# A fifth unit of the sequence transform as seven block products in six of its eight passes, with one gate/up unit more made late, and two GpSimd steps instead of four for one pair's sums

## The chip, the cores and the metric

The kernel runs on one core of a Trainium2 chip. The metric is the device time of one execution in microseconds (us), measured on the chip from outside the program. One more execution is taken by the hardware profiler; all rows of the profile and the trace quoted below come from it. Engines: PE (TensorE matmul) and PEld (its weight loads), DVE (VectorE), ACT (ScalarE), POOL (GpSimd), SP (SyncE, which here issues all the DMAs).

## The reference

A Fourier mixing layer and a GeGLU feed-forward layer, each behind a layer norm and with a residual, for one sequence of S = 2048 rows of width D = 448; the hidden width of the second layer is 1792.

```python
a = jnp.einsum("bsd,ed->bse", x, dft_hid_re)
b = jnp.einsum("bsd,ed->bse", x, dft_hid_im)
y = jnp.einsum("ts,bse->bte", dft_seq_re, a) - jnp.einsum("ts,bse->bte", dft_seq_im, b)
...
x = A_x
h = x + _A_ref(_layernorm(x, axis=-1), ...)
g = jnp.einsum("bsd,df->bsf", x, w_gate)
u = jnp.einsum("bsd,df->bsf", x, w_up)
h2 = h + einsum(gelu(g) * u, w_down)      # g and u of layernorm(h)
```

## The kernel before

All products are made in fp16 with both factors split into a high part and a low remainder (`hi_part` on ACT, `lo_part` on DVE), and three of the four products of the parts are summed: each product of the reference is three matmuls. The schedule is written out by hand or by a planner in the kernel's own code; no compiler moves an instruction.

**The Fourier stage** takes the first half. A hidden transform F(i) turns one tile of 128 rows of x (normed, split, transposed: `x_stats`, `x_rstd_steps`, `x_lo`, `x_turn`) into the tile's features: 22 matmuls of 448 columns at line 456, into two banks of a ring of PSUM (tag `"B"`, so that F(3) takes the banks that F(0) had). `feature_high` (ACT) and `feature_low` (DVE) then read the banks and write the operand tile `b0`, `b1`, ...

The sequence transform follows in 8 passes p of 8 units u. A unit U(p, u) multiplies one 512 KB block of the sequence matrix, `wr`, with the operand tiles of the pair 2u, 2u+1 and adds to the pass's four banks `acc` (line 573). A **plain** unit is 24 matmuls of 448 columns, with `ws` = high and low of all four blocks of `wr` (`seq_high`, `seq_low`, 128x1024 each). A unit of `S_UNITS` = (4, 5, 6, 7) is made from **seven block products**: 42 matmuls of 224 columns. It needs three sums of blocks (`seq_sums`, lines 517 to 521, into `wsum`), high and low of only three blocks of `wr` (`seq_parts`: 128x256 and 128x512), and high and low of the four sums (`seq_high_s`, `seq_low_s`, 128x1024, into `wss`). On the side of the features such a pair goes through a ring tile `b32` in fp32, three sums (`feature_sums`, lines 493 to 497), and high and low of seven blocks (`sums_high`, `sums_low`, 128x1568).

The stage also does other work beside the matmuls: the residual, norm and transposes of a finished pass (`seq_out`, `ffn_...`), and 12 of the 14 units f of gate/up weights (class `Weights`: sums `gu_s` at lines 642 to 648, high and low `gu_p` in four pieces, stored to a scratch in DRAM). The two others, the keys of `LATE = {4: 0, 9: 10}`, are made in the next stage by `late_prep`, in six beats from beat 0 and beat 10 (two beats in each step t, DVE sums and lows, ACT highs), stored at beat 5, and used at step t = f.

**What sets the order.** The first three F and what feeds them stand in a list by hand. All else of the Fourier stage goes through a planner, `arranged`: every piece of work is a `Task` with an engine, a cost, a due time and the tasks that it follows; a clock of 0.05 us steps gives each free engine the ready task that is due first. The order thus found is issued. A task's room in a ring is one of its conditions: `ws` has `WS_BUFS` = 4 buffers, `wss` has 2, `wr` 3, `wsum` 1. The order of units within passes p >= 1 is 0, 1, 4, 2, 5, 3, 6, 7.

**The gate/up and down stage** is 56 steps: t = 14q + f, quarter q of 512 rows. A step makes z = gate, up and their mixed products (line 1187, banks `pX`, `pY`, `pZ`) and, from q = 1 on, one step of the down product (line 1132) of the quarter before. Seven blocks of the sum over units (`dn_sums`, `dn_split`) are prepared for each down step by POOL and DVE: two adds at lines 1278 and 1279 into `dn_s`, from POOL in most steps and from DVE in steps t = 44, 46, ... 54 and 45, 51. A finished pair of output rows is drained (`dn_drain`): GpSimd adds `v` to `hr` at line 1123, two of the eight at a time (`drains[p].sums`) in the four steps t0+1 to t0+4, with t0 = 48 for the pair p = 4.

Of the kernel before, what the change touches and what calls it, by code (L numbers as in the profile page):

```python
# [1 line left out]

# [11 lines left out]
P = 128  # L14
# [18 lines left out]
def kernel(  # L33
# [287 lines left out]
    S_UNITS, WR_BUFS, WS_BUFS, WSS_BUFS, STAGE_BUFS = (4, 5, 6, 7), 3, 4, 2, 2  # L321
# [146 lines left out]
    def is_s(u):  # L468
        return u in S_UNITS
# [30 lines left out]
    def sums_high(i):  # L500
        t = bop[i] = dft.tile([P, 2, 7, HD], F16, name=f"b{i}")
        hi_part(t[:, 0], b32[i][:, 1:8])

    def sums_low(i):
        lo_part(bop[i][:, 1], b32[i][:, 1:8], bop[i][:, 0])
# [57 lines left out]
    def seq_mm(p, u, first, last):  # L563
# [4 lines left out]
        for cc in range(2):  # L568
# [7 lines left out]
            if is_s(u):  # L576
# [132 lines left out]
    plain = [u for u in ORDER if not is_s(u)]  # L709
# [6 lines left out]
    for p in range(1, N_PASS):  # L716
        slots += [("U", p, u) for u in mixed if ("U", p, u) not in early]
# [12 lines left out]
    class Task:  # L730
        def __init__(self, engine, cost, due, what, after=(), begin=0.0, lag=0.15):
            self.engine, self.cost, self.due, self.what = engine, cost, due, what
            self.after, self.begin, self.lag = [t for t in after if t], begin, lag
            self.end = None

    FIRST = 3
    COST = {"F": 4.16, "P": 4.54, "S": 4.02}
    spans = [COST["F" if s[0] == "F" else "S" if is_s(s[2]) else "P"] for s in slots]
# [7 lines left out]
    def chain(engine, costs, due, make, after=()):  # L746

        run, last = [], list(after)

        def step(first):  # L750
            if first:
                run.append(make())
            next(run[0])

        for k, cost in enumerate(costs):
            last = [add(engine, cost, due, lambda k=k: step(k == 0), after=last)]
        return last[0]
# [4 lines left out]
    def fixed(n, rank, engine, cost, what, after=(), lag=0.0):  # L762
        if n < FIRST:
            plan(n, rank, what)
            return None
        return add(engine, cost, T[n + 1], what, after=after, begin=T[n] - 1.0, lag=lag)
# [3 lines left out]
    for k, (i, i2) in enumerate(tiles_of):  # L770
        n = where["F", i]
        if k > 2:
            t = fixed(n - 10, 8, "SP", 0.1, lambda u=i // 2: x_load(u), lag=5.0)
            t = fixed(n - 7, 7, "V", 1.35, lambda i=i, j=i2: x_stats(i, j), [t])
            t = fixed(n - 6, 2, "A", 0.3, lambda i=i, j=i2: x_root(i, j), [t])
            if n - 6 < FIRST:
                fixed(n - 6, 5, "V", 0.6, lambda i=i, j=i2: x_rstd(i, j))
            else:
                t = chain("V", (0.2, 0.1, 0.1, 0.1), T[n - 5], lambda i=i, j=i2: x_rstd_steps(i, j), [t])
            t = fixed(n - 6, 5, "V", 0.15, lambda i=i, j=i2: x_bias(i, j), [t])  # L780
        for c in (i, i2):
            n = where["F", c]
            if k > 2:
                low = fixed(n - 5, 5, "A", 1.15, lambda i=c: x_norm(i), [t])
                low = fixed(n - 5, 5, "V", 0.85, lambda i=c: x_lo(i), [low])
            if k >= 2:
                turned[c] = fixed(n - 4, 2, "SP", 0.1, lambda i=c: x_turn(i), [low] if k > 2 else (), lag=5.0)
                steps[n].after += [t for t in [turned[c]] if t]
        for c in (i, i2):
            n = where["F", c]  # L790
            if not k:
                continue
            done = [steps[n]] if n in steps else []
            if is_s(c // 2):
                t = drained = add("A", 1.05, T[n + 1] + 1.5, lambda i=c: feature_high(i), after=done + ring_w[-2:][:1] * (len(ring_w) > 1))
                t = chain("V", (0.56, 0.36, 0.36), T[n + 2], lambda i=c: feature_sums(i, V), [t])
                t = add("A", 1.45, T[n + 2] + 2.0, lambda i=c: sums_high(i), after=[t])
                t = add("V", 1.7, T[n + 2] + 3.5, lambda i=c: sums_low(i), after=[t])
                ring_w.append(t)
            else:  # L800
                t = add("A", 0.95, T[n + 1] + 1.0, lambda i=c: feature_high(i), after=done)
                t = drained = add("V", 1.07, T[n + 1] + 2.5, lambda i=c: feature_low(i), after=[t])
            bop_of[c] = t
            out_of[n] = drained
    for n, s in enumerate(slots):
        if n < FIRST:
            continue
        if s[0] == "F":
            past = [m for m in out_of if m < n]
            steps[n].after += [out_of[m] for m in sorted(past)[:-1]]  # L810
        elif s[1] == 0:
            steps[n].after += [bop_of[c] for c in (2 * s[2], 2 * s[2] + 1) if c in bop_of]
# [3 lines left out]
    for g, (p, u) in enumerate(units):  # L816
# [5 lines left out]
        else:  # L822
            load = add("SP", 0.1, T[n] - 12.0, lambda p=p, u=u: seq_load(p, u), after=done_with[g - WR_BUFS], lag=5.5)
        if not g:
            done_with[g] = []
            continue
        room = [steps[where["U", *units[g - WS_BUFS]]]] if g >= WS_BUFS else []
        size = 0.9 if is_s(u) else 1.0
        high = add("A", size, T[n] - 1.6, lambda p=p, u=u: seq_high(p, u), after=[load] + room)
        low = add("V", 1.02 if is_s(u) else 1.16, T[n] - 0.4, lambda p=p, u=u: seq_low(p, u), after=[high])  # L830
        done_with[g] = [low]
        if is_s(u):
            t = chain("V", (0.6, 0.34, 0.34), T[n] - 3.0, lambda p=p, u=u: seq_sums(p, u), [load] + sums_of)
            room = [steps[s_units[-WSS_BUFS]]] if len(s_units) >= WSS_BUFS else []
            high_s = add("A", 0.98, T[n] - 1.5, lambda p=p, u=u: seq_high_s(p, u), after=[t, high] + room)
            low_s = add("V", 1.16, T[n] - 0.3, lambda p=p, u=u: seq_low_s(p, u), after=[high_s])
# [8 lines left out]
    for p in range(N_PASS):  # L845
# [10 lines left out]
        copy = add("A", 0.35, t0 + 1.0, lambda p=p: seq_copy(p), after=[steps[n - 1], load] + last_e)  # L856
        mixed_in = chain("V", (1.4 if p < 2 else 0.32, 0.64, 0.86, 0.56), t0 + 5.0, lambda p=p: seq_out(p), [copy])
        rooms[p] = [mixed_in]
        store = add("SP", 0.1, t0 + 6.0, lambda p=p: h_store(p), after=[mixed_in], lag=6.0)
        m = [add("A", 1.75, t0 + 9.0 + 4 * g, lambda q=q, j=j, g=g, p=p: ffn_moments(q, j, hp[q, j], g, junk_of(e_of[p])), after=[mixed_in]) for g in range(2)]  # L860
        t = add("A", 0.25, t0 + 14.0, lambda q=q, j=j: ffn_root(q, j), after=m)
        t = chain("V", (0.2, 0.1, 0.1, 0.1), t0 + 15.0, lambda q=q, j=j: ffn_rstd_steps(q, j), [t])
        last_e, h_done[p] = m, [store, t]
        if q < 2:
            t = add("V", 0.15, t0 + 16.0, lambda q=q, j=j: ffn_bias(q, j), after=[t])
            t = add("A", 1.35, t0 + 17.0, lambda q=q, j=j: ffn_norm_act(q, j, hp[q, j]), after=[t])
            h_done[p] = [store, t]
            for k in range(4):
                t = add("V", 0.36, t0 + 18.0 + k, lambda q=q, j=j, k=k: ffn_sums(q, j, (k,)), after=[t])
            for k in range(2):  # L870
                high = add("A", (0.65, 1.0)[k], t0 + 22.0 + k, lambda q=q, j=j, k=k: ffn_hi(q, j, (k,)), after=[t])
                t = high
            for k in range(5):
                t = add("V", (0.34, 0.87, 0.25, 0.35, 0.25)[k], t0 + 23.0 + k, lambda q=q, j=j, k=k: ffn_lo(q, j, (k,)), after=[t])
            last_e = [t]
            for k in range(4):
                add("SP", 0.1, t0 + 28.0 + k, lambda q=q, j=j, k=k: ffn_transpose(q, j, (k,)), after=[t])
# [3 lines left out]
    LATE = {4: 0, 9: 10}  # L881
# [13 lines left out]
    begin0 = 12.0  # L895
    raw, freed, stages = None, [], []
    for k, f in enumerate(order):
        gap = (at_end - 10.0 - begin0) / N_DFT
        t0 = begin0 + gap * k
        due = lambda part: t0 + gap * part  # L900
        s1 = add("V", 0.83, due(0.2), lambda f=f: gu[f].sums(True, False), after=[raw] + freed, begin=t0 - 10.0)
        s2 = add("V", 0.95, due(0.3), lambda f=f: gu[f].sums(False, True), after=[s1])
        t, lows = s2, []
        for m in range(4):
            room = stages[-STAGE_BUFS : len(stages) - STAGE_BUFS + 1]
            high = add("A", (0.55, 0.35, 0.55, 0.55)[m], due(0.35 + 0.2 * m), lambda f=f, m=m: gu[f].high(m), after=[t] + room)
            low = add("V", (0.6, 0.34, 0.6, 0.6)[m], due(0.4 + 0.2 * m), lambda f=f, m=m: gu[f].low(m), after=[high])
            stages.append(add("N", 0.0, 0.0, lambda: None, after=[low], lag=7.0))
# [694 lines left out]
```

## Time and profile before

| | |
|---|---|
| three runs | 711.84, 712.02, 713.61 us; median 712.02 |
| the profiled execution | 712.42 us |
| its span (first to last instruction on the profile) | 710.6 us |
| ACT busy, POOL busy | 56%, 28% of the span |
| Fourier stage | to about 354 us |
| gate/up of the first quarter, without down products | about 354 to 414 us |
| gate/up and down together, then the last drains | about 414 to 710.6 us |

In rows of the profile, a line number such as L573 is that of the kernel before. A busy time in a group is the sum over its instructions; "mean ns" is one instruction's.

### The profile page before, as it was taken

Reading aid. Unit: us, or ns where it says so; the run is one execution under the profiler, and the core shown is the slowest. Engines: PE = TensorE matmul, PEld = TensorE weight load, DVE = VectorE, ACT = ScalarE, POOL = GpSimd, SP = SyncE. Lnnn points to the kernel's source line nnn. Section 1 sums busy time; section 2 is a strip of 40 time slices with the busy share of each in tenths; the row PEclk is TensorE's granted clock in tenths of the full one; section 3 lists DMA queues with packets and bytes.
Section 4 is the critical chain, followed back from the end, with each engine's and each line's share of the span. In section 5 each row is a group of like instructions: output and inputs, shape, how many; then the busy total and the mean of one; then the engine's idle time right before and its main releaser. Section 6 shows DMA issues by size and latency. Waiting matters only on the chain.

```text
span 710.6 us, 15025 instructions
## 1 busy us (share of the span) xinstructions
PE 701.3 (99%) x5902; PEld 570.6 (80%) x5902; DVE 544.6 (77%) x1131; ACT 399.8 (56%) x845; POOL 197.1 (28%) x225
## 2 busy tenths in 40 slices
PE   7999999999999999999999999999999999999998
PEld 4556567777776868686888889999999999998898
DVE  6799999899988987877368667575765755887876
ACT  5587574757656665645166665555555544454432
POOL 0000000000000000002026664474664745656442
PEclk9999999999999999999999999999999999999999
DMA  9366846799988697758267745847468574445301
GB/s 330 102 151 177 209 155 200 250 206 328 245 221 284 191 245 252 258 162 318 92 238 300 271 172 171 187 165 201 176 196 188 178 208 162 176 156 178 134 28 53
DMA packets 82935, 140.64 MB, mean 198 GB/s; under 512 B 41776, under 2 KB 60464, under 8 KB 82864
## 3 DMA queue, kind: packets, MB, share of 16 engines
q1 hardware_dynamic: 82864, 139.68, 63.8%
q8 instruction: 46, 0.75, 0.4%
q14 instruction: 25, 0.20, 0.1%
HBM read 110.17 MB, written 20.19 MB: 183 GB/s over the span
## 4 chain that ended last, share of the span: by engine, by line
PE 92%; DVE 3%; ACT 2%; issue 1%; DMA 1%; SPq 0%; DVEq 0%; ACTq 0%
PE acc L573 39%; PE acc_d L1132 15%; PE pY L1187 13%; PE pZ L1187 9%; PE ab L456 9%; PE pX L1187 8%; DMA wh_raw<-in_w_hid_dram 1%; DVE dn_w L109 1%; ACT dn_w L105 1%; DVE wh_lo L111 0%; DVE hh L1197 0%; ACT c L1262 0%; DVE dn_s L1280 0%; DVE dn_s L1279 0%; ACT u L1231 0%
## 5 line engine op out<-in xcount | busy, mean ns | idle before, releaser
L1187 PEld LDWEIGHTS <-gw 128*128 128x128 f16 x2184 | 213.3, 98 | 25.4 <-issue 3.0
L573 PE MATMUL acc<-b,ws 128*128 128x448 f16 (+1 forms) x1344 | 221.9, 312 | 0.0
L573 PEld LDWEIGHTS <-ws 128*128 128x128 f16 x1344 | 130.6, 98 | 70.7
L1187 PE MATMUL pY<-hops,gw 128*128 128x256 f16 x952 | 129.1, 273 | 0.0
L1132 PE MATMUL acc_d<-wd,dn_w 128*128 128x224 f16 x1050 | 122.3, 259 | 0.0
L234 POOL TENSOR_TENSOR wd_s<-wd 128x448 f32<-128x448 f32 x7 | 8.4, 1207 | 350.2 <-DMA wr<-in_w_seq_dram 331.7
L1132 PEld LDWEIGHTS <-dn_w 128*128 128x128 f16 x1050 | 101.2, 98 | 2.8
L105 ACT ACTIVATE ws<-wr 128x256 f16<-128x256 f32 (+2 forms) x96 | 63.1, 693 | 61.4 <-PE acc L573 43.5
L573 PE MATMUL acc<-b,wss 128*128 128x224 f16 x768 | 94.5, 259 | 0.0
L1187 PE MATMUL pZ<-hops,gw 128*128 128x256 f16 x616 | 85.5, 272 | 1.9 <-DVE c L1197 1.4
L1264 POOL TENSOR_TENSOR hh<-hh,c 128x256 f32<-128x256 f32 x56 | 45.6, 815 | 145.4 <-ACT c L1262 144.9
L1187 PE MATMUL pX<-hops,gw 128*128 128x256 f16 x616 | 83.3, 273 | 0.0
L111 DVE SCALAR_TENSOR_TENSOR ws<-wr,ws 128x256 f16<-128x256 f32 (+2 forms) x96 | 72.3, 781 | 9.1 <-ACT ws L105 9.0
L573 PEld LDWEIGHTS <-wss 128*128 128x128 f16 x768 | 73.8, 98 | 0.0
L109 DVE TENSOR_TENSOR dn_w<-hh,dn_w 128x256 f16<-128x256 f32 x50 | 25.7, 515 | 50.3 <-ACT dn_w L105 50.0
L456 PEld LDWEIGHTS <-xT 128*128 128x128 f16 x352 | 34.2, 98 | 32.5 <-issue 1.4
L109 DVE TENSOR_TENSOR dn_w<-dn_s,dn_w 128x640 f16<-128x640 f32 x50 | 54.9, 1098 | 7.0 <-ACT dn_w L105 5.9
L1231 ACT ACTIVATE u<-pY 128x256 f32<-128x256 f32 x56 | 21.4, 383 | 61.7 <-PE pY L1187 61.7
L1279 POOL TENSOR_TENSOR dn_s<-hh 128x256 f32<-128x256 f32 x42 | 52.8, 1258 | 0.0
L1226 ACT ACTIVATE pY<-pX 128x256 f32<-128x256 f32 x56 | 20.6, 368 | 50.0 <-PE pX L1187 50.0
L111 DVE SCALAR_TENSOR_TENSOR wss<-wsum,wss 128x1024 f16<-128x1024 f32 x32 | 39.3, 1229 | 9.8 <-ACT wss L105 9.8
L456 PE MATMUL ab<-wh_hi,xT 128*128 128x448 f16 x224 | 45.6, 352 | 0.5 <-DVE wh_hi L435 0.2
(120 smaller groups left out, 906.5 us busy)
## 6 DMA issues: line engine op xcount, KB each, us to landing
gw<-w_dram SPq DMA_DIRECT2D x54, 896.0 KB, 4.9
wr<-in_w_seq_dram SPq DMA_DIRECT2D x64, 512.0 KB, 4.6
gu_raw<-in_w_gu_dram SPq DMA_DIRECT2D x28, 384.0 KB, 4.4
w_dram<-gu_p SPq DMA_DIRECT2D x36, 256.0 KB, 3.0
hx<-in_x_dram SPq DMA_DIRECT2D x8, 448.0 KB, 6.3
h_dram<-hx SPq DMA_DIRECT2D x8, 448.0 KB, 5.3
hr<-h_dram SPq DMA_DIRECT2D x8, 448.0 KB, 5.4
x<-in_x_dram SPq DMA_DIRECT2D x7, 448.0 KB, 6.2
```

The costliest lines, as they stand in the source:

```text
L105: A.activation(dst, src, AF.Copy, scale=scale)
L109: V.tensor_sub(dst, src, hi)
L111: V.scalar_tensor_tensor(dst, src, scale, hi, op0=ALU.mult, op1=ALU.subtract)
L234: G.tensor_sub(s[:, 2:4], t[:, 0:2], t[:, 2:4])
L456: PE.matmul(feat[i][r][:, :D], xT[i][:, kx, :], w[:, kw, r * D : (r + 1) * D], start=n == 0, stop=n == 10,)
L573: PE.matmul(banks[k][:, cols], lhs, rhs, start=k not in begun, stop=stop, skip_group_check=True)
L1132: PE.matmul(acc[k // 2][:, k % 2 * HD : (k % 2 + 1) * HD], a_of(la, a), b_of(lb, b), start=first and m == 0 and k % 2 == 0, stop=last and ...
L1187: PE.matmul(ps, w[:, wl, wa + ws, :], ops[:, m + ms, :], start=first and n == 0, stop=last and n == len(terms) - 1, skip_group_check=True,)
L1226: A.activation(self.Y, self.X, AF.Copy)
L1231: A.activation(self.u2, self.Y, AF.Copy, scale=SC)
L1264: G.tensor_mul(c22, c22, self.c12)
L1279: E.tensor_sub(s[:, 2:4], t[:, 1:4:2], t[:, 0:4:2])
```

## The change

1. Unit 3 (`MIXED`) is made as seven block products in the passes from `S_FROM` = 2 on, and stays plain in passes 0 and 1. Its two feature tiles b6 and b7 therefore go through `b32`, with eight blocks instead of seven (`k0` = 0): four plain ones, which pass 0 and 1 read, and the sums. 
2. `WS_BUFS` goes from 4 to 3. In passes from 2 on the order of the units is 0, 4, 1, 5, 3, 6, 2, 7.
3. The planner is rewritten as an event queue with a table of shifts of the due times by kind of work (`SHIFT`) and a short look-ahead (`HOLD`); work on x from the third pair on is planned too, and the hand-written head is put in another order.
4. Three gate/up units instead of two are made late, `LATE = {4: 0, 8: 8, 12: 15}`, and a late unit is stored in step t = f, after that step's first beat, instead of at its sixth beat. Eleven instead of twelve are made in the Fourier stage.
5. In the down stage, for the pair p = 4 only, the eight GpSimd sums are made four in step t0+1 and four in step t0+3 (t0 = 48). The second of two DVE `dn_sums` of block 7 moves from step 51 to 53, its split from 52 to 54.

```diff
-    S_UNITS, WR_BUFS, WS_BUFS, WSS_BUFS, STAGE_BUFS = (4, 5, 6, 7), 3, 4, 2, 2
+    S_UNITS, WR_BUFS, WS_BUFS, WSS_BUFS, STAGE_BUFS, MIXED, S_FROM = (4, 5, 6, 7), 3, 3, 2, 2, 3, 2
...
-    def is_s(u):
-        return u in S_UNITS
+    def is_s(u, p=N_PASS):
+        return u in S_UNITS or u == MIXED and p >= S_FROM
...
     def sums_high(i):
-        t = bop[i] = dft.tile([P, 2, 7, HD], F16, name=f"b{i}")
-        hi_part(t[:, 0], b32[i][:, 1:8])
+        k0 = i // 2 != MIXED
+        t = bop[i] = dft.tile([P, 2, 8 - k0, HD], F16, name=f"b{i}")
+        hi_part(t[:, 0], b32[i][:, k0:8])
...
-            if is_s(u):
+            if is_s(u, p):
                 for a, o, k, half in PRODUCTS:
+                    o += u == MIXED
...
     for p in range(1, N_PASS):
+        if p == S_FROM:
+            mixed = [0, 4, 1, 5, 3, 6, 2, 7]
...
-            self.engine, self.cost, self.due, self.what = engine, cost, due, what
+            self.engine, self.cost, self.due, self.what = engine, cost, due + SHIFT.get(kind, 0.0), what
...
+    SHIFT = {"copy": 30.3, "fhigh": -61.6, "fhighp": -4.0, "flow": 6.9, "fsum": 4.8, "guhi": -6.2, "gulo": 2.0,
...
+    HOLD = (1.58, 5.3)
...
-    LATE = {4: 0, 9: 10}
+    LATE = {4: 0, 8: 8, 12: 15}
...
-    begin0 = 12.0
+    begin0 = 16.6
...
-        gap = (at_end - 10.0 - begin0) / N_DFT
+        gap = (at_end - 0 - begin0) / N_DFT
...
+            t = able[e][0][2]
+            soon = [w[2].at for w in waiting[e] if e in "VA" and w[0] < now + HOLD[0] * t.cost and w[2].due + HOLD[1] < t.due]
+            if soon:
+                free[e] = min(soon)
+                continue
...
+    x_stats(2, 3)
+    x_root(2, 3)
+    feature_mm(0, range(4, 6))
...
-    feature_high(0)
-    feature_low(0)
-    x_rstd(a, b)
-    x_bias(a, b)
...
-    for n, t in enumerate((3 * NF + 3, 3 * NF + 9)):
+    for n, t in enumerate((3 * NF + 3, 3 * NF + 11)):
...
         for n in range(4):
-            at(side, (t0 + 1 + n, 3), lambda p=p, n=n: drains[p].sums((2 * n, 2 * n + 1)))
+            after = 1 + n if p != 4 else 1 + n // 2 * 2
+            at(side, (t0 + after, 3), lambda p=p, n=n: drains[p].sums((2 * n, 2 * n + 1)))
...
         if k == 5:
-            gu[f].store()
             gw[f] = gu[f].w
...
             late_prep(2 * t)
+            if t in LATE:
+                gu[t].store()
```

Three places show how it moves instructions. The first is DVE in the head, around the low part of the first feature tile (`b0`, read from the banks `ab0_0` and `ab0_1`); `st_x10` and `mv_x10` are the statistics of the x tiles 10 and 11, `r_x10` the reciprocal of their deviation. Before:

```order
L353 BN_STATS st_x10_364<-x5_181 128x6
L353 BN_STATS st_x11_365<-x5_181 128x6
L355 BN_AGGR mv_x10_363<-st_x10_364 128x2
L355 BN_AGGR mv_x10_363<-st_x11_365 128x2
L111 SCALAR_TENSOR_TENSOR b0_372<-ab0_0_232,b0_372 128x448
L111 SCALAR_TENSOR_TENSOR b0_372<-ab0_1_233,b0_372 128x448
```

And the same place now, where the four rows of the pair 10, 11 stand just ahead of those shown:

```order
L354 BN_STATS st_x4_390<-x2_373 128x6
L354 BN_STATS st_x5_391<-x2_373 128x6
L356 BN_AGGR mv_x4_389<-st_x4_390 128x2
L356 BN_AGGR mv_x4_389<-st_x5_391 128x2
L354 BN_STATS st_x12_401<-x6_375 128x6
L354 BN_STATS st_x13_402<-x6_375 128x6
L356 BN_AGGR mv_x12_400<-st_x12_401 128x2
L356 BN_AGGR mv_x12_400<-st_x13_402 128x2
L141 RECIPROCAL r_x10_411<-sd_x10_398 128x2
L142 TENSOR_SCALAR r_x10_411<-mv_x10_382 128x2
L112 SCALAR_TENSOR_TENSOR b0_345<-ab0_0_231,b0_345 128x448
L112 SCALAR_TENSOR_TENSOR b0_345<-ab0_1_232,b0_345 128x448
```

The statistics of two more pairs (tiles 4, 5 and 12, 13) and two short steps now stand between those of the first pair and the low part of `b0`.

The second is ACT in pass 3, between the norm of a finished pass (`xn_h1_0`) and the start of pass 4. `ws3_6` is the high part of three blocks of unit 6 of pass 3, `wss3_6` that of its four sums, `gu_p7_2` a piece of a gate/up unit. Before:

```order
L105 ACTIVATE wss3_5_2456<-wsum3_5_2398 128x1024
L253 ACTIVATE xn_h1_0_2466<-hx2_1578,nb_h1_0_2463,r_h1_0_2453 128x448 x2
L105 ACTIVATE ws3_3_2497<-wr3_3_2393 128x1024
L105 ACTIVATE ws3_6_2502<-wr3_6_2383 128x256
L105 ACTIVATE ws3_6_2502<-wr3_6_2383 128x512
L105 ACTIVATE gu_p7_2_2513<-gu_s7_2297 128x512
L105 ACTIVATE wss3_6_2516<-wsum3_6_2495 128x1024
```

And now:

```order
L106 ACTIVATE wss3_3_2459<-wsum3_3_2441 128x1024
L106 ACTIVATE gu_p6_1_2466<-gu_raw6_2141 128x256
L106 ACTIVATE ws3_6_2511<-wr3_6_2411 128x256
L106 ACTIVATE ws3_6_2511<-wr3_6_2411 128x512
L254 ACTIVATE xn_h1_0_2521<-hx2_1498,nb_h1_0_2517,r_h1_0_2461 128x448 x2
L106 ACTIVATE gu_p6_2_2531<-gu_s6_2335 128x512
L106 ACTIVATE wss3_6_2579<-wsum3_6_2519 128x1024
```

Unit 3 of pass 3, which had its one `ws` of 128x1024 between the sums of units 5 and 6, now has sums of its own, so that three `wss` (units 5, 3, 6) follow one another; gate/up is a unit behind.

The third is POOL in the down stage in steps 49 to 51 (`hr4` is the output of the pair p = 4, `x2` two instructions). Before:

```order
L1123 TENSOR_TENSOR hr4_8044<-hr4_8044,v0_4_8603 128x224 x2
L1264 TENSOR_TENSOR hh3_7947<-hh3_7947,c12_49_8689 128x256
L1278 TENSOR_TENSOR dn_s38_8750<-hh2_6627 128x256
L1279 TENSOR_TENSOR dn_s38_8750<-hh2_6627 128x256
L1123 TENSOR_TENSOR hr4_8044<-hr4_8044,v1_4_8604 128x224 x2
L1264 TENSOR_TENSOR hh3_7947<-hh3_7947,c12_50_8788 128x256
L1278 TENSOR_TENSOR dn_s39_8843<-hh2_6627 128x256
L1279 TENSOR_TENSOR dn_s39_8843<-hh2_6627 128x256
L1123 TENSOR_TENSOR hr4_8044<-hr4_8044,v0_4_8603 128x224 x2
```

And now:

```order
L1138 TENSOR_TENSOR hr4_8197<-hr4_8197,v0_4_8756 128x224 x2
L1138 TENSOR_TENSOR hr4_8197<-hr4_8197,v1_4_8757 128x224 x2
L1279 TENSOR_TENSOR hh3_8100<-hh3_8100,c12_49_8842 128x256
L1293 TENSOR_TENSOR dn_s38_8905<-hh2_6780 128x256
L1294 TENSOR_TENSOR dn_s38_8905<-hh2_6780 128x256
L1279 TENSOR_TENSOR hh3_8100<-hh3_8100,c12_50_8943 128x256
L1293 TENSOR_TENSOR dn_s39_8996<-hh2_6780 128x256
L1294 TENSOR_TENSOR dn_s39_8996<-hh2_6780 128x256
L1138 TENSOR_TENSOR hr4_8197<-hr4_8197,v0_4_8756 128x224 x2
```

Four sums of `hr4` come ahead of the product `c12_49` of step 49 and none ahead of that of step 50.

More of the change, by code (lines that the diff above doesn't have):

```diff
@@ L744, in add, with chain @@
         return tasks[-1]
-    def chain(engine, costs, due, make, after=()):
+    def chain(engine, costs, due, make, after=(), kind=None):
         run, last = [], list(after)
@@ L755, in chain @@
         for k, cost in enumerate(costs):
-            last = [add(engine, cost, due, lambda k=k: step(k == 0), after=last)]
+            last = [add(engine, cost, due, lambda k=k: step(k == 0), after=last, kind=kind)]
         return last[0]
@@ L781 @@
         for c in (i, i2):
             n = where["F", c]
[L783 to L793, printed above, removed]
+            done = [steps[n]] if n in steps else [add("N", 0.0, 0.0, lambda: None, begin=(-1.8, -1.0, 0.1)[n])]
@@ L794 @@
             if is_s(c // 2):
[L795 to L798, printed above, removed]
+                t = drained = add("A", 1.05, T[n + 1] + 1.5, lambda i=c: feature_high(i), after=done + ring_w[-2:][:1] * (len(ring_w) > 1), kind="fhigh")
@@ L921, in arranged @@
+    t = fixed(len(slots) - 14, 9, "SP", 0.1, lambda: down_load(0), last_e, lag=6.0, kind="dload")
+    fixed(len(slots) - 8, 9, "G", 4.0, lambda: down_sums(0), [t], kind="dsum")
     def arranged():
[L923 to L951 removed]
@@ new lines, in arranged @@
+        free = {"V": -4.1, "A": -0.9, "G": 0.0, "N": -9.0, "SP": -9.0, "PE": 0.0}
+        last = None
+        for n in range(FIRST, len(slots)):
+            steps[n].after = [a for a in steps[n].after if a] + ([last] if last else [])
+            last = steps[n]
+        left, next_of, begun = {}, {}, []
+        waiting = {e: [] for e in free}
+        able = {e: [] for e in free}
+        everything = tasks + [steps[n] for n in range(FIRST, len(slots))]
+        number = {id(t): k for k, t in enumerate(everything)}
@@ L952, in arranged @@
+        begun.sort(key=lambda t: t.start)
+        number = {id(steps[n]): n for n in steps}
+        begun = [(t.start, number.get(id(t), t)) for t in begun]
         return begun
```

237 lines of the change are left out of this document (121 added, 116 removed).

## The prediction, made before the changed kernel ran

> **What bounds the kernel now.** I begin with the page: the busy times, then the chain of work that ended last.
>
> ```profile
> PE 701.3 (99%) x5902; PEld 570.6 (80%) x5902; DVE 544.6 (77%) x1131; ACT 399.8 (56%) x845; POOL 197.1 (28%) x225
> ```
>
> TensorE is busy for 701.3 us of a span of 710.6, so the time moves only with the matmuls' own length or with holes put into their row. The chain, from the Fourier stage (start, length, what):
>
> ```profile
> 14.49 1.00 DVE wh_lo L111
> ...
> 28.99 4.54 PE acc L573 x24
> ...
> 63.04 4.03 PE acc L573 x42
> ...
> 100.60 252.41 PE acc L573 x1956
> ```
>
> A plain unit takes 4.54 us, one of seven block products 4.03, and from 100.60 to 353.0 nothing but matmuls stands in the chain. The question is whether DVE, which the change gives more to do, can still keep ahead. By stretch (busy time of PE, PEld, DVE, ACT, POOL; granted clock; DMA):
>
> ```profile
> 46.39:100.60 54.21, 54.21 (x330) 31.92 (x328) 51.50 (x110) 36.42 (x61) 0.00 (x0) 1.00 0.68 189
> 100.60:227.00 126.40, 126.40 (x971) 93.59 (x970) 114.74 (x232) 82.55 (x156) 0.00 (x0) 1.00 0.80 235
> 227.00:354.00 127.00, 127.00 (x999) 96.20 (x997) 94.74 (x184) 64.97 (x122) 4.01 (x3) 1.00 0.71 222
> 354.00:382.00 28.00, 27.98 (x257) 24.91 (x256) 18.77 (x37) 18.42 (x45) 10.20 (x11) 1.00 0.71 263
> 382.00:416.00 34.00, 33.89 (x313) 30.28 (x311) 24.76 (x43) 22.48 (x54) 21.00 (x24) 1.00 0.71 254
> 640.00:680.00 40.00, 38.64 (x369) 35.47 (x367) 29.40 (x55) 20.08 (x52) 19.39 (x22) 1.00 0.39 139
> ```
>
> PE is full in the first three at clock 1.00, and DVE has 2.7, 11.7 and 32.3 us to spare there. The fourth and fifth rows are the steps in which two gate/up units are made late: PE lost 0.13 us. The last holds the pair p = 4: PE lost 1.36 us of 40.
>
> **The block products.** Unit 3 goes from 4.54 to 4.03 us in six passes: 6 x 0.51 = **-3.06 us**. The matmuls are of the form that 32 units of the kernel have already.
>
> One rule speaks against it. The Trainium skill, "TensorE: Matmul & The Clock Gate", section "Back-to-back issue gap", gives a sustained spacing of 81 ns at 128 columns and 131 ns at 512; on a line between them, an estimate, 24 matmuls of 448 would take 2.9 us and 42 of 224 would take 3.9, and six exchanges would cost 5.9 us more instead of 3.06 less. The trace has 4.54/24 = 189 ns and 4.03/42 = 96 ns, so the measured spacing here goes with the columns and the rule doesn't hold.
>
> **What DVE pays for it.** First what a unit of seven products has: all its sums and the low part of the sums (tile `wsum`, DVE busy from 0 to 354, x128 for 32 units), and the lows of three blocks where a plain unit has one of 128x1024 (count, busy us, mean ns, idle before).
>
> ```profile
> 0.00:354.00 354.00, 88.17 (x128) 1.00 0.73 220
> ...
> L111 DVE SCALAR_TENSOR_TENSOR ws<-wr,ws 128x1024 f16<-128x1024 f32 x32 | 39.1, 1220 | 7.9 <-ACT ws L105 7.9
> ...
> L111 DVE SCALAR_TENSOR_TENSOR ws<-wr,ws 128x512 f16<-128x512 f32 x32 | 22.4, 699 | 0.1
> ...
> L111 DVE SCALAR_TENSOR_TENSOR ws<-wr,ws 128x256 f16<-128x256 f32 x32 | 13.5, 423 | 1.1 <-ACT ws L105 1.1
> ```
>
> 88.17/32 + 0.699 + 0.423 - 1.220 = 2.66 us more per unit, 15.9 in six. For the two feature tiles:
>
> ```profile
> L109 DVE TENSOR_TENSOR b<-b,b 128x1568 f16<-128x1568 f32 x8 | 14.3, 1789 | 0.6 <-ACT b L105 0.3
> ...
> L111 DVE SCALAR_TENSOR_TENSOR b<-ab,b 128x448 f16<-128x448 f32 x16 | 9.2, 616 | 1.5 <-ACT b L105 1.5
> ...
> L493 DVE TENSOR_TENSOR b<-b 128x448 f32<-128x448 f32 x8 | 5.0, 621 | 0.6 <-ACT b L105 0.6
> ...
> L495 DVE TENSOR_TENSOR b<-b 128x224 f32<-128x224 f32 x8 | 3.1, 387 | 0.0
> L497 DVE TENSOR_TENSOR b<-b 128x224 f32<-128x224 f32 x8 | 3.1, 386 | 0.0
> ```
>
> With eight blocks for seven: 1.789 x 8/7 + 0.621 + 0.387 + 0.386 - 2 x 0.616 = 2.2 per tile, 4.4 for both. One gate/up unit of the twelve leaves the stage (tile `gu_s`, then the lows made straight from `gu_raw`):
>
> ```profile
> 0.00:354.00 354.00, 38.25 (x72) 1.00 0.73 220
> ...
> L111 DVE SCALAR_TENSOR_TENSOR gu_p<-gu_raw,gu_p 128x512 f16<-128x512 f32 x12 | 8.2, 685 | 0.0
> ...
> L111 DVE SCALAR_TENSOR_TENSOR gu_p<-gu_raw,gu_p 128x256 f16<-128x256 f32 x12 | 5.0, 418 | 0.0
> ```
>
> (38.25 + 8.2 + 5.0)/12 = 4.3. Net 15.9 + 4.4 - 4.3 = 16 us, against 2.7 + 11.7 + 32.3 = 46.7 spare between 46 and 354. So the total fits; ACT, with 18 and 44 us to spare in the second and third stretch, too. The crowded place is 100 to 227: of the new work 4.4 and up to three units at 2.66, 12.4 us, fall to before 227, and 11.7 are free. Gate/up has to give way there, and it can: its units run a little slower all along, and it has 32 us of spare DVE behind. SP's queue gains no DMA from it; it loses one unit's loads and stores.
>
> Whether single units are late is read from how far ahead DVE works. The group of the sums' highs on ACT, then one low of the sums, and its first use:
>
> ```profile
> L105 ACT ACTIVATE wss<-wsum 128x1024 f16<-128x1024 f32 x32 | 33.6, 1050 | 16.3 <-DVE wsum L521 13.1 <-PE acc L573 3.1
> ...
> 226.91 1.23 DVE L111 SCALAR_TENSOR_TENSOR wss<-wsum,wss 128x1024 f16<-128x1024 f32 x1 [0.52 <-ACT wss L105]
> ...
> 234.03 0.45 PE L573 MATMUL acc<-b,wss 128*128 128x224 f16 x3
> ```
>
> The low ends at 228.14, 5.9 us before PE needs it. Two things shorten this lead. `ws` has three buffers instead of four, so one unit can be ready and another in the making while a third runs: two units, 8.1 to 9.1 us at most, still more than 5.9. And units 5, 3, 6 now follow one another with only two `wss`: the high part of unit 6's sums waits for the end of unit 5. From there PE has unit 3, 4.03 us, and 0.57 us of unit 6 (six matmuls) before it asks for `wss`: 4.6 us. The high of 128x1024 takes 1.05, the low 1.23, the hand-overs some 0.3: 2.6. Behind the waiting high on ACT stand the parts of units 2 and 7, which have longer. Two us are left, and one unlucky DVE instruction ahead of the low (the longest are 1.8 to 2.0) eats them. Bounds: 0 (all hidden) to +3 (0.5 in each of six passes); I take **+0.3**, near the row's 5.9.
>
> **The head.** DVE and PE in the head:
>
> ```profile
> 15.15 0.34 PE L418 MATMUL xT_ps<-ident,xs 128*128 128x128 f16 x3 [0.98 <-ACT xs L105]
> ...
> 20.55 1.14 DVE L353 BATCH_NORM_STATS2 st_x<-x 128x6 f32<-128x448 f32 x2
> 21.61 0.29 DVE L355 BATCH_NORM_AGGREGATE mv_x<-st_x 128x2 f32<-128x6 f32 x2
> 22.70 1.16 DVE L111 SCALAR_TENSOR_TENSOR b<-ab,b 128x448 f16<-128x448 f32 x2 [0.80 <-ACT b L105]
> ...
> 24.66 2.81 PE L456 MATMUL ab<-wh_hi,xT 128*128 128x448 f16 x14
> ```
>
> F(3) writes the banks that the lows of `b0` read, so it cannot start before these are done: 23.86 before, and it started at 24.66, when PE came to it. Now three pairs of statistics stand ahead of them, 3 x 1.43 = 4.3 us, and two steps of some 0.15. The tiles 2 and 3 share their statistics' small steps now, so DVE can come to this place earlier than 20.55: I take 19.5 to 20.2. Then `b0` is done at 25.3 to 26.0. PE could be there sooner than before: the list puts the low of `wh` behind the transposes of the second tile, whose 0.98 us of waiting may go in part; I put its readiness at 23.9, 0.75 earlier. Bounds: -0.75 (`b0` in time) to +1.7 (`b0` at 26.1 and 0.25 to hand over). I take **+0.7**, F(3) at 25.4, the early end, since `b0`'s first bank is free 0.58 us before its second and PE can begin on it. What comes behind starts later by as much.
>
> **Late units.** The two late units cost PE at most the 0.13 us above, and their DVE work runs slower there (GpSimd is busy beside it):
>
> ```profile
> 379.15 0.68 DVE L642 TENSOR_TENSOR gu_s<-gu_raw 128x384 f32<-128x384 f32 x1
> ...
> 383.30 0.83 DVE L648 TENSOR_TENSOR gu_s<-gu_raw,gu_s 128x256 f32<-128x256 f32 x1
> ...
> SPq L697 <- DVE gw L111: 9.7, 2, 6.5
> ```
>
> A third unit adds about 5 us of DVE work to a stretch with 9 spare in 28 and 9 in 34. In proportion 0.07, at most one stalled step of 1 us: **+0.2**. The moved stores free SP, which stood up to 6.5 us at a store that waited for a low part, with the loads of later units queued behind; those loads were in time anyway, so I count nothing.
>
> **The down stage.** Waits first, then DVE's and POOL's adds:
>
> ```profile
> PE pZ L1187 <- DVE c L1197: 1.4, 2, 0.7
> ...
> 633.85 0.41 DVE L1279 TENSOR_TENSOR dn_s<-hh 128x256 f32<-128x256 f32 x1
> ...
> 646.97 0.88 DVE L1279 TENSOR_TENSOR dn_s<-hh 128x256 f32<-128x256 f32 x1
> ...
> 646.06 1.50 POOL L1123 TENSOR_TENSOR hr<-hr,v 128x224 f32<-128x224 f32 x2
> ```
>
> The two waits of 0.7 are nearly all of the 1.36 us that PE loses in 640 to 680 (I find the holes at 647.8 and 661.3, in steps 50 and 52). DVE's `dn_s` adds take 0.41 alone and 0.88 beside `hr`; two of them make DVE 0.94 late. Now steps 50 and 52 have no `hr` sums, and step 51, where no DVE sums are left, and 49 have no such pair beside the four. So both waits go: **-1.3**, bounds 0 and -1.4.
>
> **Sum.** -3.06 + 0.3 + 0.7 + 0.2 - 1.3 = -3.16 us on the profiled execution of 712.42 us: 709.26. That execution lies 0.40 above the median of the runs, 712.02; against that, **708.9 us**.
>
> **Rivals.**
>
> 1. *Single stalls in the passes.* The `wss` of unit 6 comes 0.4 us late in each of the six passes, because a long DVE instruction stands in front. For it: only 2.0 us of room. Against it: leads of 5.9 elsewhere. Six times 0.4: 711.3.
> 2. *DVE sets the pace before 227.* This is the slower side. If gate/up doesn't give way, the 12.4 us added there come as a block; the lead of 5.9 is eaten and PE waits for the other 6.5: 715.4. It decides from the point where DVE's extra work between two lows exceeds the lead. For it: 51.50 of 54.21 and 114.74 of 126.40 are used already. Against it: gate/up can move to where 32 us are free, and the planner counts DVE's time.
> 3. *The down stage keeps its holes*, because four `hr` sums in a row hold up other work of POOL: the 1.3 stays, 710.2.
> 4. *The weight loads set the pace of the new units.* One takes 98 ns:
>
> ```profile
> L573 PEld LDWEIGHTS <-wss 128*128 128x128 f16 x768 | 73.8, 98 | 0.0
> ```
>
> 42 x 98 ns = 4.12 us a unit; the gain falls to 6 x 0.42 = 2.5 us: 709.5. The 32 units at 4.03 speak against it.
>
> 5. *The head gains.* `b0` is in time and PE keeps the 0.75: 1.45 us better than my sum, and with no stall, 707.0.
>
> **How the numbers follow.** Forecast 0.58, with a range of its own of 707.4 to 710.4; stalls 0.16; DVE's pace 0.11; holes kept 0.09; head 0.04; loads 0.02. The predicted time is the forecast's. From 706.6 to 712.6 leaves out rival 2, the far end of rival 1, and little of rival 5: 0.16 in all. A measurement can tell 0.3%, 2.1 us, from no change: faster is below 709.9, slower above 714.1. Faster: 0.50 of the forecast's 0.58, 0.04 of the holes kept, rivals 4 and 5, together 0.60. Slower: 0.10, nearly all of rival 2. The rest, 0.30, is within.
>
> **What would show it.** The windows 100 to 227 and 227 to 354 with PE full, and the chain with one piece of PE from about 100 on, ending about 2.0 us earlier than 353.0 (-3.06 + 0.7 + 0.3): the blocks right. PE waiting for `wss` or `ws` there: rival 1 or 2, told apart by whether it is 0.4 once a pass or grows in a row of units. F(3) after 25.4: the head worse than taken. The waits of `pZ` for `c` gone and PE above 39.5 of 40 in steps 49 to 54: the down stage right. What would make the prediction wrong is a hole in PE that I have no row for, in the rewritten order's first passes above all.

## The result, and the profile after

| | before | changed |
|---|---|---|
| runs, us | 711.84, 712.02, 713.61, 713.83 | 707.58, 707.74, 707.90, 708.99 |
| median, us | 712.82 | 707.82 |
| profiled execution, us | 712.42 | 707.58 |
| its span, us | 710.6 | 705.8 |

The ratio is 0.9938, with a 95% interval of 0.9925 to 0.9951: 5.0 us faster by the medians (before has a fourth run here beside the three shown first), 4.8 by the two profiled executions. The predicted 708.9 lies 1.1 us above the measured median, which is inside the range given.

The page's row of busy times, of the changed kernel:

```profile
PE 698.5 (99%) x6010; PEld 581.1 (82%) x6010; DVE 561.0 (79%) x1160; ACT 407.4 (58%) x858; POOL 197.2 (28%) x225
```

TensorE works 2.8 us less with 108 matmuls more, and DVE 16.4 us more: the exchange that was described. The chain (start, length, what) shows where the rest came from:

```profile
19.52 1.07 DVE st_x L354 x2
...
23.43 1.07 DVE b L112 x2
24.54 4.13 PE ab L457 x21
28.67 4.54 PE acc L576 x24
...
100.28 249.32 PE acc L576 x2064
```

The long piece of matmuls is 249.32 us instead of 252.41, 3.09 shorter, and still one piece: DVE did keep up. It ends at 349.60 instead of 353.01, and of these 3.41 us 0.32 were there when U(0,0) began (28.67 for 28.99). By stretch (PE, PEld, DVE, ACT, POOL busy; clock; DMA):

```profile
46.39:100.60 54.21, 54.21 (x330) 31.93 (x328) 50.13 (x99) 37.95 (x58) 0.00 (x0) 1.00 0.65 147
100.60:227.00 126.40, 126.40 (x1023) 98.37 (x1021) 120.23 (x250) 83.34 (x158) 0.00 (x0) 1.00 0.80 231
227.00:352.00 125.00, 125.00 (x1066) 102.54 (x1065) 105.60 (x198) 68.47 (x130) 3.48 (x3) 1.00 0.69 232
352.00:380.00 28.00, 27.80 (x254) 24.61 (x253) 20.14 (x38) 19.77 (x48) 11.25 (x12) 1.00 0.73 253
380.00:414.00 34.00, 34.00 (x316) 30.58 (x314) 28.08 (x49) 23.78 (x56) 22.67 (x24) 1.00 0.78 262
636.00:676.00 40.00, 40.00 (x385) 37.10 (x383) 27.71 (x59) 20.41 (x53) 20.04 (x24) 1.00 0.41 139
```

DVE's added work is mostly in the third row: between 100.60 and 227 it rose by 5.5 us, behind 227 by 10.9 in a stretch 2 us shorter. Gate/up did give way to where room was: DVE's work on `gu_s` fell from 17.31 to 12.90 us between 100.60 and 227, and rose from 12.60 to 14.30 between 227 and 354. The last row, with the pair p = 4, has no hole left.

Between the end of the Fourier stage and the last steps without down products the kernels keep their distance (the same matmuls of the first quarter, before and after):

```profile
410.78 1.20 PE pX L1187 x11
```

```profile
407.44 1.20 PE pX L1202 x11
```

3.34 us there, against 3.41 at the end of the Fourier stage. So the span's 4.8 us are: head 0.3, blocks 3.1, late units -0.1, and 1.5 behind 414.

### The profile page after: what moved, and what is told of

It is laid out like the page before. It is cut to its first block, busy times and chain, and to the rows that moved or that the text cites. A ratio compares the mean times of both kernels' runs of the same rounds, so it can differ in the third digit from the quotient of the medians.

```text
span 705.8 us, 15279 instructions
## 1 busy us (share of the span) xinstructions
PE 698.5 (99%) x6010; PEld 581.1 (82%) x6010; DVE 561.0 (79%) x1160; ACT 407.4 (58%) x858; POOL 197.2 (28%) x225
## 4 chain that ended last, share of the span: by engine, by line
PE 94%; DVE 2%; ACT 1%; DMA 1%; issue 1%; SPq 0%; DVEq 0%; ACTq 0%
PE acc L576 38%; PE acc_d L1147 15%; PE pY L1202 14%; PE pZ L1202 9%; PE pX L1202 9%; PE ab L457 8%; DMA x<-in_x_dram 1%; DVE st_x L354 1%; DVE dn_w L110 0%; ACT dn_w L106 0%; SPq L429 0%; DVE hh L1212 0%; ACT xn_h L254 0%; DVE wd L112 0%; ACT xT L420 0%
## 5 line engine op out<-in xcount | busy, mean ns | idle before, releaser
L576 PE MATMUL acc<-b,ws 128*128 128x224 f16 (+1 forms) x1308 | 208.9, 304 | 0.0
L576 PEld LDWEIGHTS <-ws 128*128 128x128 f16 x1308 | 126.9, 98 | 57.5
L576 PE MATMUL acc<-b,wss 128*128 128x224 f16 x912 | 112.2, 259 | 0.0
L576 PEld LDWEIGHTS <-wss 128*128 128x128 f16 x912 | 87.7, 98 | 0.0
L110 DVE TENSOR_TENSOR dn_w<-hh,dn_w 128x256 f16<-128x256 f32 x50 | 25.3, 506 | 53.3 <-ACT dn_w L106 52.9
L112 DVE SCALAR_TENSOR_TENSOR wss<-wsum,wss 128x1024 f16<-128x1024 f32 x38 | 46.4, 1221 | 8.5 <-ACT wss L106 8.3
L106 ACT ACTIVATE wss<-wsum 128x1024 f16<-128x1024 f32 x38 | 39.9, 1050 | 22.3 <-DVE wsum L524 11.9
```

The lines of the kernel that those rows point to most:

```text
L106: A.activation(dst, src, AF.Copy, scale=scale)
L110: V.tensor_sub(dst, src, hi)
L112: V.scalar_tensor_tensor(dst, src, scale, hi, op0=ALU.mult, op1=ALU.subtract)
L576: PE.matmul(banks[k][:, cols], lhs, rhs, start=k not in begun, stop=stop, skip_group_check=True)
```

## The experiments

Eleven runs are edits of the changed kernel, the twelfth is that kernel again. Times are compared with its 707.82, and the first profile's span of 705.8 with theirs. The kernel before ran beside each of them as well: its medians there were 712.21 to 712.55, for 712.82 beside the 707.82. So a difference of medians below some 0.6 us says nothing by itself, and the rows of the profile have to decide.

**1. The blocks alone.** Unit 3 plain in every pass; nothing else undone.

```diff
-    S_UNITS, WR_BUFS, WS_BUFS, WSS_BUFS, STAGE_BUFS, MIXED, S_FROM = (4, 5, 6, 7), 3, 3, 2, 2, 3, 2
+    S_UNITS, WR_BUFS, WS_BUFS, WSS_BUFS, STAGE_BUFS, MIXED, S_FROM = (4, 5, 6, 7), 3, 3, 2, 2, -1, 2
```

> Unit 3 plain in every pass, all else as in the changed kernel (order of units, three ws buffers, three late units, drains). Theory (the blocks are worth 6 x 0.51 us and DVE hides all of its added work): 3.1 us longer than the changed kernel's 707.8, 710.9; matmuls of the Fourier stage without a hole after 100 us in both. Rival (part of the gain comes from DVE's work falling out elsewhere, or the new units cost something hidden): a difference under 2.5 or over 3.7 us.

710.49 us (709.88 to 712.06, 8 runs), span 708.9: 2.7 more by the medians, 3.1 by the spans. The chain of this run:

```profile
100.26 252.41 PE acc L576 x1956
```

The piece is before's to the hundredth. The blocks are worth 3.09 us in it, and the span's 3.1 leaves no part that comes or goes elsewhere. The order of units and the three `ws` buffers, which this run keeps, cost nothing in the piece.

**2. One pass more.** `S_FROM` = 1.

```diff
-    S_UNITS, WR_BUFS, WS_BUFS, WSS_BUFS, STAGE_BUFS, MIXED, S_FROM = (4, 5, 6, 7), 3, 3, 2, 2, 3, 2
+    S_UNITS, WR_BUFS, WS_BUFS, WSS_BUFS, STAGE_BUFS, MIXED, S_FROM = (4, 5, 6, 7), 3, 3, 2, 2, 3, 1
```

> Unit 3 as seven products in seven passes, from pass 1 on, with the new order of units from pass 1 on. Theory (DVE has 6.2 us spare of 126.4 between 100.6 and 227 and units are 1.0 to 6 us ahead): the 2.7 us of DVE work more fit in, 0.5 us shorter than the changed kernel (707.3). Rival (DVE sets the pace there): matmuls wait for ws or wss in passes 1 and 2, +1 to +3 us (709 to 711).

708.13 us (707.37, 708.13, 709.31). Two pieces of its chain, its window and its wait of PE:

```profile
101.64 42.33 PE acc L576 x348
...
162.29 189.06 PE acc L576 x1597
```

```profile
100.00:227.00 127.00, 126.44 (x1041) 100.01 (x1040) 121.93 (x247) 83.11 (x159) 0.00 (x0) 1.00 0.75 227
```

```profile
PE acc L576 <- DVE ws L112: 0.4, 1, 0.4
```

The matmuls of the passes take from 101.64 to 351.35, 249.71 us, where the changed kernel takes 249.32. So the 0.51 that the seventh exchange should save is lost, and 0.39 more; the window shows 0.56 of it as idle, at the wait before 162.29. The theory's half us is not there, and the rival's price was smaller than it said: this is the edge, with DVE at 122 of 127 us. (The execution began late for another reason, told at the end.)

**3. The head: `b0` in front of the third pair's statistics** (tiles 12 and 13).

```diff
             t = fixed(n - 7, 7, "V", 1.35, lambda i=i, j=i2: x_stats(i, j), [t], kind="xstat")
+            t.due += 16.0 * (k == 4)
```

> The statistics of the x tiles 12 and 13 are made after the low part of b0 instead of before it, all else as in the changed kernel. Theory (F(3) waits only for b0's low, by 0.38 and 0.18 us): F(3) starts at 23.6 to 23.7 instead of 24.0, U(0,0) 0.5 us earlier than 28.67, and the whole is 0.5 us shorter (707.3). Rival (the transposes of the x tiles 10 and 11 end last then): F(10) starts late and U(0,0)'s gain is lost before 42 us, time unchanged at 707.8.

708.79 us (708.36 to 709.28), span 707.0. Chain and wait of PE:

```profile
28.27 4.54 PE acc L576 x24
...
67.80 8.50 PE ab L457 x44
```

```profile
PE ab L457 <- DMA xT<-xs: 1.5, 1, 1.5
```

U(0,0) did begin 0.4 earlier than in the first profile, which is less than its scatter (run 12). The F behind U(0,5) then waited 1.46 us for its transpose. By the order of the tile pairs (0, 1, 5, 2, 6, 3, 7, 4) that is F(6): the rival's mechanism, though not at F(10), nor at F(12), which I took it for when I wrote the expectation of run 10. What this pair's place in front of `b0` costs can't be told from the scatter; putting it behind costs 1.5 us at F(6).

**4. The GpSimd sums in four steps again**, DVE's move kept.

```diff
-            after = 1 + n if p != 4 else 1 + n // 2 * 2
+            after = 1 + n
```

> The GpSimd sums of the pair p = 4 in four steps again (two in each), the move of DVE's sums from step 51 to 53 kept. Theory (DVE's sums are slow beside GpSimd's): in steps 50 and 52 the sums take 0.88 instead of 0.41 us each, pZ waits 0.7 us for c twice, +1.4 us (709.2). Rival (the move from 51 to 53 freed DVE enough): within 0.3 of 707.8.

709.12 us (708.95 to 709.34, 4 runs), span 707.1. Window, then the wait:

```profile
636.00:676.00 40.00, 38.65 (x368) 35.45 (x367) 28.30 (x54) 19.96 (x51) 19.44 (x22) 1.00 0.40 139
```

```profile
PE pZ L1202 <- DVE c L1212: 1.3, 2, 0.7
```

Both waits are back, 1.3 us longer: the two steps are what removes them.

**5. DVE's sums in step 51 again**, the two GpSimd steps kept.

```diff
-    for n, t in enumerate((3 * NF + 3, 3 * NF + 11)):
+    for n, t in enumerate((3 * NF + 3, 3 * NF + 9)):
```

> DVE's second sums of block 7 in step 51 again, its split in step 52, the GpSimd sums of p = 4 in two steps kept. Theory (it is the sums beside GpSimd that cost): step 51 now has DVE sums beside four GpSimd sums, 0.88 each instead of 0.41, and step 52 a double split without GpSimd sums: one wait of pZ for c of 0.7 us, 708.5. Rival (the double split in the crowded step is what cost): both waits are back, 709.2. Rival (either move alone is enough): 707.8.

707.64 us (707.14, 707.23, 708.04, 709.17), span 705.4. PE in the window, DVE's second add in step 51:

```profile
636.00:676.00 40.00, 40.00 (x385) 37.02 (x383) 29.43 (x59) 20.52 (x53) 20.34 (x24) 1.00 0.39 139
```

```profile
648.19 0.88 DVE L1294 TENSOR_TENSOR dn_s<-hh 128x256 f32<-128x256 f32 x1
```

The add is slow, 0.88, and PE does not wait in this step. So that part of the change does nothing here, and the theory, which gave the slow adds of any step a price, fell. Before's trace had it too: in step 51 (652.17) they took 0.88 without a wait. What makes step 51 bear it wasn't tried.

**6. Two late units instead of three.**

```diff
-    LATE = {4: 0, 8: 8, 12: 15}
+    LATE = {4: 0, 9: 10}
```

> Two gate/up units made late (4 and 9) instead of three; twelve are made in the Fourier stage, 4.3 us of DVE work more there. Theory (DVE's spare time of 4, 6 and 19 us in the three stretches covers it): no hole after 100 us, the late stage 0.1 shorter, 707.7. Rival (DVE sets the pace before 227): holes before 227 that add 1 to 4 us, 709 to 712.

714.87 us (714.33 to 715.60, 4 runs), 7 us longer, and slower than the kernel before: ratio 1.0039 (1.0019 to 1.0058). Window and PE's waits:

```profile
100.00:227.00 127.00, 121.99 (x967) 93.68 (x965) 115.07 (x229) 77.49 (x144) 0.00 (x0) 0.99 0.69 211
```

```profile
PE acc L576 <- DVE b L110: 2.7, 2, 2.5
PE acc L576 <- DVE ws L112: 1.6, 1, 1.6
PE acc L576 <- DVE wss L112: 0.4, 2, 0.3
```

PE lost 5.0 us in this window, but DVE worked less in it than in the changed kernel (115.07 for 120.83 of the same 127): it is not simply full. (Some 1.7 us of the 7 went to a low clock behind the longest hole, told at the end.) In that hole, 2.46 us up to 118.19, PE waited for the low part of a feature tile, and the chain has the lows of four other pieces on DVE just ahead of it (start, length, what):

```profile
113.14 2.15 DVE ws L112 x3
115.30 1.14 DVE wss L112
116.44 1.71 DVE b L110
```

The next runs take order and load apart.

**7. Shifts and look-ahead off**, three late units.

```diff
-    SHIFT = {"copy": 30.3, "fhigh": -61.6, "fhighp": -4.0, "flow": 6.9, "fsum": 4.8, "guhi": -6.2, "gulo": 2.0,
...
-    HOLD = (1.58, 5.3)
+    SHIFT = {}
+    HOLD = (0.0, 5.3)
```

> The table of shifts of the due times empty and the look-ahead off; the rest of the planner and all other edits as in the changed kernel. Theory (spare DVE time alone hides the added work): within 1 us of 707.8. Rival (the order is what hides it): PE waits for ws and wss between 46 and 227 us, 3 us or more longer (711 and up).

708.14 us (707.30, 708.14, 709.36), span 705.5; the chain:

```profile
99.95 249.32 PE acc L576 x2064
```

The table of shifts gains nothing that can be seen: with plain due times the piece takes the same 249.32 us without a hole. With three late units, spare DVE time is enough.

**8. Two late units, unit 3 plain** (edits 6 and 1).

> Two gate/up units made late and unit 3 plain in every pass: the 20 us of DVE work for the blocks are gone from the run with two late units, which took 714.9. Theory (DVE's work before 227 was too much for it): no hole after 100 us, 3.1 us above the changed kernel, 710.9, that is 4 us faster than with the blocks. Rival (the tuned order puts gate/up in front of the last feature tiles, whatever the load): the holes at 113 to 118 and 207 us stay, 714 or more.

712.38 us (711.71 to 715.54, 8 runs), span 710.1. One wait is left:

```profile
PE acc L576 <- DVE wss L112: 0.8, 1, 0.8
```

That is 1.9 us above run 1 (1.2 by the spans, of which 0.9 is this hole: the passes take from 100.70 to 354.04, 253.34 us for 252.41). It lies between theory and rival: without the blocks most of run 6's holes go, but not all.

**9. Two late units, shifts off** (edits 6 and 7).

> Two gate/up units made late, blocks in six passes, and the table of shifts empty and the look-ahead off. Theory (load): the same work has to be done before 227, holes of 3 us or more stay, 711 or more. Rival (order): by the plain due times the holes go, 707.5 to 708.5.

708.84 us (708.79 to 708.96, 3 runs), span 707.0. PE waits once in the passes:

```profile
237.76 0.27 PE L576 MATMUL acc<-b,wss 128*128 128x224 f16 x1 [1.20 <-DVE wss L112]
```

So run 6's 7 us are mostly the order: the same work, by plain due times, is 6.0 us faster. The load itself costs 1.5 us by the spans (707.0 for run 7's 705.5; 0.7 by the medians of three runs each), nearly all of it at this hole: the passes take from 100.31 to 350.99, 250.68 us for 249.32. Theory and rival were each right in part.

**10. `b0` earlier, more gently**: `t.due += 10.0` in edit 3.

> The statistics of the x tiles 12 and 13 behind the low of b0 and behind the bias of tiles 10 and 11, but two DVE instructions earlier than in the run that put them far back. Theory (their place in front of b0 costs 0.5 us, and only being 7 us late cost F(12) 1.5): U(0,0) at 28.2, no wait for a transpose behind it, the block after 100 us begins 0.4 earlier, 707.4. Rival (any place behind b0 makes a later F late): one wait of F for a transpose of 0.5 to 1.5 us, 708 to 709.

708.20 us (707.99, 708.20, 708.80). PE's wait:

```profile
PE ab L457 <- DMA xT<-xs: 0.9, 1, 0.9
```

Now it is F(10) that waits, and U(0,0) began at 28.7, no earlier than in the first profile. That is the rival's mechanism; the 0.4 us of the medians lie within the scatter, so that this head has no room to give is likely and not shown.

**11. Four late units, seven passes, shifts off.**

```diff
-    LATE = {4: 0, 8: 8, 12: 15}
+    LATE = {4: 0, 7: 6, 10: 12, 13: 18}
```

> Four gate/up units made late (4, 7, 10, 13), ten in the Fourier stage; unit 3 as seven products in seven passes; table of shifts empty, look-ahead off. Theory (DVE's cover is what limits the blocks; another 4.3 us of DVE work less before 349 pays for 2.7 more): no hole after 100 us, 0.5 us less in the passes, 0.1 to 0.2 more in the late stage, a start of F(10) up to 0.4 late: 0.2 to 0.4 below the changed kernel. Rival (the late stage, where DVE is at 20 of 28 and 28 of 34 us, is full): holes there of 1 us or more, 708.5 or more.

724.47 us (723.73 to 726.11, 5 runs), 17 us longer. Two windows and PE's waits:

```profile
100.00:227.00 127.00, 123.20 (x1016) 97.28 (x1015) 116.94 (x241) 81.29 (x152) 0.00 (x0) 1.00 0.75 215
...
414.00:500.00 86.00, 79.31 (x739) 72.21 (x737) 53.98 (x112) 43.43 (x107) 45.60 (x52) 0.96 0.65 198
```

```profile
PE pZ L1197 <- DVE hh L1207: 6.2, 4, 5.2
PE acc L576 <- DVE wss L112: 3.9, 4, 1.5
PE pX L1197 <- DMA gw<-w_dram: 1.4, 1, 1.4
```

A fourth unit, at these beats, is too much for what comes behind the Fourier stage, and by far more than the rival's 1 us. The largest piece there has another cause than DVE's load: in the longest wait, 5.16 us up to 431.20, DVE's `hh` had itself waited 5.58 us, by the profile for the store of a late unit (`w_dram<-gw`). The passes lost 3.8 us before 227 as well, and their matmuls ended at 356.31, 6.7 us later than in the changed kernel, which less gate/up work didn't prevent; two things differ from run 7 here, so which one did it isn't shown.

**12. The changed kernel again.**

> The changed kernel itself, beside the other on one chip. Theory: 707.7 within 0.5, the Fourier stage's matmuls from 100 us on 249.3 us without a hole, the start of U(0,0) anywhere from 28.1 to 28.7, since seven runs of this head start between these. Rival (the first profile's head was a lucky one): U(0,0) at 29 or later, 708.5 or more.

707.41 us (707.00 to 709.23, 6 runs) against 712.34 before on the same chip: ratio 0.9931 (0.9919 to 0.9943). Its chain:

```profile
28.89 4.54 PE acc L576 x24
...
100.50 249.32 PE acc L576 x2064
```

U(0,0) began at 28.89, outside the 28.1 to 28.7 that I had named. With the same hand-written head it began at 28.67, 28.65, 28.32, 28.12, 28.22, 29.09 and 28.89 in the profiles of the changed kernel and of runs 1, 4, 5, 6, 8 and 12: a scatter of 1 us, in which before's 28.99 lies too. What makes this start scatter isn't shown.

No variant beat the changed kernel by more than its scatter.

## Why the prediction was right, and where a step was off

**The blocks: right, and shown.** -3.06 was forecast, -3.09 measured, and run 1 gives it back alone. The rule that spoke against it, in the Trainium skill's "TensorE: Matmul & The Clock Gate", section "Back-to-back issue gap", doesn't hold for the new units either: by it the piece would have grown by 5.9 us, and it shrank by 3.09.

**DVE's cover: right in kind, +0.3 taken, 0 measured.** The net 16 us came out as 15.0 (50.13 + 120.23 + 105.60 = 275.96 of DVE between 46 and 352, for 51.50 + 114.74 + 94.74 = 260.98 between 46 and 354). The crowded place was named rightly and so was its room, "two us": in pass 3 the low of unit 6's sums, and PE's first use.

```profile
199.13 1.22 DVE L112 SCALAR_TENSOR_TENSOR wss<-wsum,wss 128x1024 f16<-128x1024 f32 x1 [0.98 <-ACT wss L106]
```

```profile
202.44 0.45 PE L576 MATMUL acc<-b,wss 128*128 128x224 f16 x3
```

The low ends at 200.35, 2.09 us ahead; nothing ate that room, so rival 1 did not happen. Rival 2's mechanism exists but not where I put its point. I priced it by load alone, at 715.4 when gate/up doesn't give way. Runs 6, 7 and 9 show that order decides as much: one gate/up unit more costs 1.5 us in one order and 7 in the other. A reading beside it was wrong, and nothing hung on it: ACT's 18 and 44 us to spare are those of the first and second stretch (54.21 - 36.42 and 126.40 - 82.55), not of the second and third; and rival 5's sum comes to 707.1.

**Late units: the sign was right, the reason was half of it.** I counted the third late unit as a cost of 0.2, and the late stage did lose 0.1. What I missed is what it buys: without it the passes stall, by 1.4 us even in the kinder order. My sum had it only as 4.3 us less of net work, and by its own argument, "the total fits" in 46.7 us, 20 us would have fitted as well as 16.

**The head: wrong, +0.7 taken, -0.3 measured.** The step that failed is "Now three pairs of statistics stand ahead of them, 3 x 1.43 = 4.3 us". DVE in the changed head:

```profile
19.45 1.14 DVE L354 BATCH_NORM_STATS2 st_x<-x 128x6 f32<-128x448 f32 x2
...
20.72 1.12 DVE L354 BATCH_NORM_STATS2 st_x<-x 128x6 f32<-128x448 f32 x2
...
21.97 1.12 DVE L354 BATCH_NORM_STATS2 st_x<-x 128x6 f32<-128x448 f32 x2
...
23.33 1.15 DVE L112 SCALAR_TENSOR_TENSOR b<-ab,b 128x448 f16<-128x448 f32 x2
```

The pairs follow each other every 1.26 us, since an instruction's record overlaps the next by some 0.1. Before's rows showed this already: the statistics at 20.55 last 1.14, to 21.69, and the next row begins at 21.61. `b0` was done at 24.48, not 25.3 to 26.0. PE had its work ahead of F(3) done at 23.62 (I had 23.9) and lost only two short waits there, 0.38 and 0.18. The profile puts the second down to `b0`, the first to a high part on ACT (`ws`) that ended within 0.1 us of `b0`'s first bank:

```profile
24.00 0.35 PE L457 MATMUL ab<-wh_hi,xT 128*128 128x448 f16 x1 [0.38 <-ACT ws L106]
24.54 2.62 PE L457 MATMUL ab<-wh_hi,xT 128*128 128x448 f16 x13 [0.18 <-DVE b L112]
```

That PE waits for `b0`, and that it can begin on the first bank ahead of the second, was right, though whether the first bank's wait was for `b0` can't be told. The lower bound, which is rival 5's case, was nearer than the value that I took. Whether the head gained at all isn't settled: 0.3 us is less than the scatter found in run 12.

**The down stage: right, -1.3 taken, -1.5 measured.** 1.36 us of it is the window that is now full, and run 4 shows the two GpSimd steps as the cause. I had named the move of the DVE sums beside it; run 5 shows that it is worth nothing.

By the profiled executions the sum was 1.7 us short (-3.16 for -4.84): 1.0 of it is the head's, 0.3 the stalls', 0.2 the down stage's and 0.1 the late units'. All four were taken too high, so that no error made good another. That the forecast time lies only 1.1 us above the measured one is partly luck: it was counted from before's median of 712.02, which is 712.82 with the fourth run; the forecast change of 3.1 us is 1.9 short of the measured 5.0.

## What to carry to other kernels

Work that is taken off the bounding engine counts in full as long as its price lies on an engine that is early: measure by how many us a result is ready before its first use, place by place, and the sum follows. Put instructions of a busy engine end to end by the distance of their starts, not by the sum of their durations. An order tuned for one load can be worth nothing at that load and cost several us at the next, so the plain order belongs among the experiments.

## What the runs showed of the hardware

In run 6 PE stood idle for 2.46 us, and then ran at half clock. PE's busy time in slices of 1 us, then the granted clock and the DMA columns:

```profile
116.00:117.00 1.00, 0.00 (x0) 1.00 0.92 344
117.00:118.00 1.00, 0.00 (x0) 1.00 0.98 339
118.00:119.00 1.00, 0.81 (x6) 0.69 1.00 366
119.00:120.00 1.00, 1.00 (x7) 0.50 0.92 364
120.00:121.00 1.00, 1.00 (x8) 0.50 0.95 369
121.00:122.00 1.00, 1.00 (x7) 0.60 0.21 72
122.00:123.00 1.00, 1.00 (x7) 1.00 0.25 83
```

The low clock lasted about 3.3 us, so that the hole cost some 1.7 us beyond its own length. A hole of 1.60 us in the same run (207 to 209), of 1.46 in run 3 and of 1.20 in run 9 changed nothing in the clock. The Trainium skill, "TensorE: Matmul & The Clock Gate", section "What's actually happening", has half clock after an idle window of about 3.4 us, and full clock again after about 3.4 us of sustained work. The second agrees with the 3.3 here; for the first, an idle time of 2.46, with another of 0.25 some 2.5 us before it, was already enough.

Single executions of kernels without such a hole had a mean clock of 0.997 or 0.998, and most of them were 1 to 2 us longer than their like. In the one of them that was profiled, run 2's, the half clock lay in the head, from about 10.3 to 13.6 us, and U(0,0) began at 30.03.

GpSimd and DVE: DVE's add of two operands in SBUF took 0.41 us alone and 0.88 beside GpSimd's adds in the profiles of before and of runs 4 and 5. The Trainium skill, "SBUF — State Buffer", section "Who interferes with whom", says that such a DVE instruction contends with a GpSimd one that reads SBUF; the rows agree.
